# An S4 convolution and a GeGLU layer in one kernel: dt's broadcast, the order of exponentials, the table of a tanh, and a new order of steps

## The chip, the core and the metric

The kernel runs on one core of a Trainium2 chip. The core has a matrix engine (TensorE, PE in the profile, its weight loads as PEld), a vector engine (VectorE, DVE), an activation engine (ScalarE, ACT), GpSimd (POOL) and SyncE (SP), which here issues nearly all DMAs. Each engine works off its own instructions in order and waits on semaphores of the others. The metric is the device time of one execution in microseconds; times are medians of several runs. A time "at 165.68" is counted from the start of the profiled execution's span.

## The reference

Two branches are computed from the same input `x = u` (2048 positions, 640 channels) and mixed by a gate:

```python
g = sigmoid((x * gate_w).sum(-1, keepdims=True))
# branch a: a long convolution, one kernel of 2048 taps per channel
dt = exp(log_dt)[:, None]; A = A_re + 1j*A_im
P = exp((dt*A)[:, :, None] * l)                  # channel, state, tap
K = einsum("dn,dnl,dn->dl", C, P, dt*B).real
y = irfft(rfft(pad(u)) * rfft(pad(K)))[:L] + u * Dskip
# branch b: the feed-forward layer, 1728 hidden features
b = (gelu(x @ w_gate) * (x @ w_up)) @ w_down     # tanh form of gelu
out = g * y + (1 - g) * b
```

## The kernel before, in words

**Powers and taps.** The 2048 taps of the convolution kernel are products of a coarse and a fine factor, `eA` (21 exponents) and `eB` (32 exponents), for 128 states in partitions. Their sizes are exponentials of `a32[:, 0]` = dt times A's real part and of `a32[:, 1]`, which is twice that: `exps` (line 362) takes exponents in pairs (v, 2v) in one instruction where both are wanted, and alone where not. Their angles are phases made on DVE (`trig`, tile `ph`) and sines made on ACT (tile `T`). `ktable` multiplies size and angle on DVE; `contract` sums over the states on PE (tiles `cv`, evicted to `Kraw`), and `gather` turns the result round through memory (`Kd`) into `KTt`. The five parts of 128 channels are worked in groups of 2, 2 and 1.

**The start.** `scaled_a` (line 326) loads the exponential's table, spreads `log_dt` over 128 partitions by two matmuls with a row of ones, takes dt as the exponential of this, brings both halves of A into place by ten matmuls each with the identity, and multiplies. `turn_x` turns the first half of x on PE; the second half is brought by transposing loads that SP issues (`load_x`).

**Feed-forward.** `ffn_up` (line 619) makes a block of both projections, 10 matmuls of 512 columns, in one of two PSUM tiles `gu`; its copy to one of three tiles `GU` is done by ACT or DVE, and `send` stores it to `GUd` in memory. There are 54 such blocks, put between the steps of the tap tables. Later `glu_load`, `gelu`, `glu` (a multiply on DVE) and `down` (28 matmuls per block of 128 positions) take them up again. The down weights `Wd` are loaded in two halves; the first half lies where part 4's `Kraw` was.

**Convolution.** It goes through Fourier windows as matmuls: `u_forward` and `k_forward` (evicted by steps V and Q to `Uf` and `Kf`), `products` on DVE (`Ma`, `Mb`, `Tp`), `inverse` on PE, and `unfold`, which adds the skip term and branch b, scales by the gate and stores. All PSUM tiles `cv` are two buffers.

**The gate.** `gate` (line 649) makes 16 columns of logits, and takes the sigmoid as a tanh on ACT followed by a short chain on DVE, which gives `g32` and `rat`.

**What sets the order.** `ORDER` (line 36) is a list of 530 steps written out by hand: a letter for the kind, then part or row block, then index, and for evictions the engine (A for ACT, D for DVE, M for half each). `u` is the next up-projection, `p` its copy, `o` its store, `W` the next weight load, `e` exponentials, `t` phases and sines, `q` tap tables, `c` contraction, `C` its eviction, `w` the gather, `K`/`Q` and `U`/`V` the forward windows and their evictions, `P` products, `I`/`J` the inverse, `D`/`d` the down-projection and its eviction, `l`/`b` loads of the stored blocks, `G`/`g` gelu and multiply, `h` the gate, `L` a half of the down weights, `m` a Fourier matrix. The steps are issued in this order, and a scheduler then places each engine's instructions where it finds room, unless a dependency holds them. `table` chains all ACT instructions that need a table in the order of the list, `first` does the same for the first steps on DVE.

```python
b32 = pp.tile([N, D], FP32, name="b32")
def scaled_a():
    table(... InstLoadActFuncSet(..., act_func_set_id=6))
```

Of the kernel before, what the change touches and what calls it, by code (L numbers as in the profile page):

```python
# [9 lines left out]
ALU = mybir.AluOpType  # L10
# [23 lines left out]


ORDER = """
s a M W e04 i2 x01D e02 n M W e00 e03 i0 x00D x02D x10D e13 x12A u e01 pD u pA v o o x11A S0 S1 e05 u W r0 pD u pD u
e15 o pA o u pD u o e12 pA i1 r1 u u pD u m m o u t04 u o y3 u pD u o pD o o pD pD o o u r2 u pD W y2 pD o o k pD u o
e10 pA u W u e11 o e14 t05 y4 u !0 pA pA pA o o o t07 u pA q05 u u u pA pA W o pA o o t02 pA t06 q07 u t00 o q06 u y0
pA t01 t03 q01 pD q00 o y1 o o u pA q02 o W q04 q03 u pD t14 o u c02 t10 t16 u pA o c00 pD u pD c10 C00A c01 u !1 pA o  # L40
C02A c11 W o o q10 u C01D C10A m u C11D w0 u pA pA c12 C12A w1 o m u W pA m pA o o u u o t11 pA q11 o W u t17 t15 e24
u pA u o pD u o pD u pA W o o pD q17 u pD u e21 q15 u W o pA e22 u e25 q16 e23 o e20 pD o o pD o pA t13 o q14 t12 q12
m m u q13 c20 C20A u c22 pA c21 C21D t20 c30 m m c32 !2 C32A C22A pA C30A t21 u c31 m f0 m w2 C31A o q20 t22 F0P t23
U00 U03 U01 V01A u w3 o V03A V00A q22 q23 pD o U02 h K00 Q00D pA K02 q21 Q02D K03 u K01 V02A Q03A c40 C40A Q01D f1 pA
o !3 W b00 F1P c41 l00 G00 u L0 C41D pA c42 o l01 C42A l10 b01 w4 g00 b10 b11 P00 P01 U10 V10A u P02 U12 V12A f2 pA u
o o pA U13 K10 K12 Q12A Q10A V13A P03 u K11 G01 U11 pA L1 V11A F2A K13 Q13A Q11A K20 D00 g01 D01 Q20A P10 K22 K21 Q21A
U20 d01A U22 V20A Q22A P11 d00A l11 U23 V22A K23 D02 V23A f3 l20 Q23A d02D G10 g10 F3A I00 U21 U30 P12 V30A U33 o o
D03 G11 V21A U31 D10 I10 V33D d10A f4 D11 b20 d03A V31A U32 z00D g11 d11A D13 K30 d13A I01 z10A F4A Q30A K32 b21 V32A
K31 Q32A P20 P21 D12 l21 d12A G20 P22 Z00A P23 Q31A l30 Z01A g20 D20 U40 G21 z01A P13 d20D K40 I11 g21 V40A K42 z11A
Q40A K41 b30 G30 D21 I20 U42 D23 Q41A d23A K33 d21A K43 Q33M l31 Q43A D22 d22A P30 Z02A g30 U41 b31 Q42M G31 g31 D30  # L50
V41D I21 U43 V42A z20D V43D d30A P31 P32 D32 z21A d32A I30 P33 P40 z30A D31 J33 j33D d31A D33 J32 d33A Z03A P41 Z11A
P42 J41 j41A J40 P43 j40A j32A Z12A Z10A Z20D J43 J42 j43D Z21D j42A Z22M Z23D Z13D
"""


# [1 line left out]
def kernel(  # L57
# [18 lines left out]
    nc = tc.nc  # L76
# [12 lines left out]
    NM = 4  # L89
    DH = D // 2  # L90
    tt = nc.vector.tensor_tensor
# [55 lines left out]
    ident = cp.tile([128, 128], BF16, name="ident")  # L147
# [81 lines left out]
    ldt = pw.tile([1, D], BF16, name="ldt")  # L229
    ones = pw.tile([1, N], BF16, name="ones")  # L230
# [93 lines left out]
    b32 = pp.tile([N, D], FP32, name="b32")  # L324

    def scaled_a():
        table(nc.scalar.add_instruction(mybir.InstLoadActFuncSet(
            name=nc.get_next_instruction_name(), engine=mybir.EngineType.Activation, act_func_set_id=6)))
        pL = psC.tile([128, 2, 512], FP32, name="cv")
        pL = pL[:].rearrange("p e x -> p (e x)")[:, 0:D]  # L330
        for sl in (slice(0, 512), slice(512, D)):
            nc.tensor.matmul(pL[:, sl], lhsT=ones[:], rhs=ldt[:, sl], start=True, stop=True)
        table(nc.scalar.activation(out=dtb[:], in_=pL, func=ACT.Exp))
        pA = []
        for t in (Are_n, Aim_n):
            p = psF.tile([128, 2, 512], FP32, name="gu")
            pA.append(p[:].rearrange("p e x -> p (e x)")[:, 0:D])
            col = pA[-1].rearrange("n (p k) -> n k p", k=KT_)
            for k in range(KT_):
                n = (511 - k) // KT_ + 1  # L340
                for sl in (slice(0, n), slice(n, 128)):
                    nc.tensor.matmul(col[:, k, sl], lhsT=t[:, k], rhs=ident[:, sl], start=(k == 0), stop=True,
                                     skip_group_check=True)
        first(tt(out=a32[:, 0], in0=pA[0], in1=dtb[:], op=ALU.mult))
        first(nc.vector.tensor_scalar(out=a32[:, 1], in0=a32[:, 0], scalar1=2.0, scalar2=None, op0=ALU.mult))  # L345
        first(nc.vector.scalar_tensor_tensor(out=b32[:], in0=pA[1], scalar=TURN / (2.0 * math.pi), in1=dtb[:],
                                             op0=ALU.mult, op1=ALU.mult))
# [14 lines left out]
    def exps(p0, np_, y):  # L362

        dA, dB = tabs[p0 // 2]
        sl = slice(p0 * DP, (p0 + np_) * DP)
        if y == 0:
            nc.gpsimd.memset(dB[:, 0:np_, :, SLOT[0], :], 1.0)
        if y == 4:
            nc.gpsimd.memset(dA[:, 0:np_, 0, :], 1.0)
        jobs = jobs_b[6 * y:6 * y + 6] if y < 4 else jobs_a[7 * (y - 4):7 * (y - 3)]  # L370
        for xs, scale in jobs:
            n = len(xs)
            xsl = slice(xs[0], xs[-1] + 1, max(1, xs[-1] - xs[0]))
# [6 lines left out]
            table(nc.scalar.activation(out=dst, in_=src, func=ACT.Exp, scale=float(scale)))  # L380
# [174 lines left out]
    def dinv(m, r, e):  # L555
        return DFT[:, 2 + m // 2].rearrange("p r f -> p (r f)")[:, 512 * (m % 2) + 256 * r + 128 * e:][:, 0:128]
# [92 lines left out]
    def gate():  # L649
        pG = psC.tile([128, 2, 512], FP32, name="cv")  # L650
        for x in range(16):
            for kt in range(KT_):
                nc.tensor.matmul(pG[:, 0, x:x + 1], lhsT=xt_tile(kt, x // 4, x % 4), rhs=gwc[:, kt:kt + 1],
                                 start=(kt == 0), stop=(kt == KT_ - 1))
        glog = cp.tile([128, 16], BF16, name="glog")
        nc.scalar.copy(out=glog[:], in_=pG[:, 0, 0:16])
        gth = cp.tile([128, 16], FP32, name="gth")
        table(nc.scalar.activation(out=gth[:], in_=glog[:], func=ACT.Tanh, scale=0.5))
        g_bf = cp.tile([128, 16], BF16, name="g_bf")
        nc.vector.tensor_scalar(out=g_bf[:], in0=gth[:], scalar1=0.5, scalar2=0.5, op0=ALU.mult, op1=ALU.add)  # L660
# [133 lines left out]
    def products(part, j):  # L794
        mp = pools["mp"]
        if j == 0:
            pst[part] = (mp.tile([128, 2, 2, 2, 512], BF16, name="Ma"),
# [2 lines left out]
        Ma, Mb, T = pst[part]  # L800
# [10 lines left out]

        def join(M, c0, c1):
            tt(out=M[:, c0:c1, 0, 0], in0=M[:, c0:c1, 0, 0], in1=M[:, c0:c1, 1, 1], op=ALU.subtract)
            tt(out=M[:, c0:c1, 0, 1], in0=M[:, c0:c1, 0, 1], in1=M[:, c0:c1, 1, 0], op=ALU.add)

        last = part == NP - 1
        if j == 0:
# [18 lines left out]
    def inverse(part, c0, nc_):  # L836
# [12 lines left out]
        o = DP * (part - ZG[z][0])  # L849
        pY = psC.tile([128, 2, 512], FP32, name="cv")  # L850
        cs = slice(c0 % 2, c0 % 2 + nc_)
        for c in range(c0, c0 + nc_):
            for r in range(2):
                for e in range(2):
                    for m in range(NM):
                        nc.tensor.matmul(pY[:, c % 2, 256 * r + 128 * e:256 * r + 128 * (e + 1)], lhsT=dinv(m, r, e),  # L856
                                         rhs=pst[part][c // 2][:, c % 2, 0, r, 128 * m:128 * (m + 1)],
                                         start=(m == 0), stop=(m == NM - 1))
# [32 lines left out]
    pst = {}  # L891
# [44 lines left out]
    for step in ORDER.split():  # L936
# [3 lines left out]
        eng = step[-1]  # L940
# [101 lines left out]
        elif kind == "Q":  # L1042
            k_out(x, y, eng)
        elif kind == "P":
            products(x, y)
        elif kind == "l":
            glu_load(x, y)
        elif kind == "b":
# [47 lines left out]
```

## Time and profile before

| What | Value |
|---|---|
| Median of 3 runs | 319.92 us (319.89 to 319.99) |
| The profiled execution | 320.46 us |
| its span, first to last instruction | 318.5 us |
| PE busy | 292.6 us (92%) |
| DVE busy | 295.1 us (93%) |
| ACT busy | 249.1 us (78%) |
| DMA | 51.40 MB, 161 GB/s on the mean |
| table loads on ACT | 9, of 1.28 us each |

The profiled execution is one run with the hardware profiler; its 320.46 us hold the span and 1.96 us around it. The chain of waits goes back from the last instruction to what released each step; its shares are PE 38%, DVE 27%, ACT 18%, DMA 8%. A matmul's end is modelled, so that matmuls in a row overlap in the list: one row of 10 matmuls tells more by its length over all than by the time of one. In a timeline row stand the start, the length, the engine, the line, the operation, the tiles (written <- read), the shapes, the count, and in brackets how long the engine was idle before it and what ended that.

### The profile page before, as it was taken

The numbers are of one execution on the slowest core, as the hardware profiler recorded it, in microseconds if no ns is written. First come the engines' busy times: TensorE is split into PE (matmuls) and PEld (weight loads), VectorE is DVE, ScalarE is ACT, GpSimd is POOL, SyncE is SP. The second block draws the span as 40 slices with busy tenths as digits, with TensorE's granted clock in tenths as the row PEclk, the third lists the DMA queues.
The fourth block names the chain that finished last, engine by engine and source line by source line (L and its number), as shares of the span: only waits on it lengthen the run. The fifth ranks groups of instructions, "written<-read, shape, count | busy, mean of one in ns | idle before, by whom it ended". The sixth has DMA issues, their size and how long they took to land.

```text
span 318.5 us, 6270 instructions
## 1 busy us (share of the span) xinstructions
PE 292.6 (92%) x2432; PEld 182.0 (57%) x2463; DVE 295.1 (93%) x416; ACT 249.1 (78%) x351; POOL 14.4 (5%) x78
## 2 busy tenths in 40 slices
PE   4399999999999999999998889999989999999994
PEld 3243444444555444454475667676677877687773
DVE  3985999999998999999889999999989999999964
ACT  5989999999898899998999768926596738542750
POOL 7720000000000000000000000000000000000000
PEclk9999999999999999999999999999999999999999
DMA  7997456656627795454594699847826352900233
GB/s 220 167 245 220 155 182 209 214 161 215 182 71 164 205 278 182 154 111 127 104 283 137 117 321 232 233 115 182 228 63 172 87 147 70 263 2 0 56 97 82
DMA packets 102543, 51.40 MB, mean 161 GB/s; under 512 B 44081, under 2 KB 95730, under 8 KB 102514
## 3 DMA queue, kind: packets, MB, share of 16 engines
q1 hardware_dynamic: 102256, 50.48, 59.2%
q0 software_dynamic: 256, 0.53, 0.6%
q8 instruction: 19, 0.31, 0.4%
q14 instruction: 10, 0.08, 0.1%
q10 hardware_dynamic: 2, 0.00, 0.0%
HBM read 30.86 MB, written 18.16 MB: 154 GB/s over the span
## 4 chain that ended last, share of the span: by engine, by line
PE 38%; DVE 27%; ACT 18%; DMA 8%; issue 7%; SPq 1%; DVEq 0%; ACTq 0%
PE gu L788 17%; DVE ph L408 5%; PE cv L856 4%; PE gu L627 4%; DVE GU L127 3%; DVE ph L416 3%; PE cv L712 3%; PE cv L729 3%; ACT GU L123 3%; DVE sB L584 2%; DMA Wd<-in_B_w_down_dram 2%; DMA HT<-GUd 2%; ACT T L424 2%; PE cv L878 2%; DVE eB L585 2%
## 5 line engine op out<-in xcount | busy, mean ns | idle before, releaser
L627 PE MATMUL gu<-xT,W 128*128 128x512 bf16 x523 | 121.8, 382 | 4.0 <-ACT GU L123 1.4
L627 PEld LDWEIGHTS <-W 128*128 128x128 bf16 x540 | 52.2, 98 | 70.1 <-issue 12.5
L788 PE MATMUL gu<-Wd,HT 128*128 128x320 bf16 x448 | 64.4, 299 | 0.8 <-DMA Wd<-in_B_w_down_dram 0.8
L788 PEld LDWEIGHTS <-HT 128*128 128x128 bf16 x448 | 43.5, 98 | 18.6 <-issue 0.9
L424 ACT ACTIVATE T<-ph 128x1024 bf16<-128x1024 int16 (+3 forms) x40 | 46.4, 1196 | 2.6 <-DVE ph L408 1.5
L123 ACT CAST GU<-gu 128x1024 bf16<-128x1024 f32 (+1 forms) x33 | 32.3, 981 | 4.0 <-PE gu L627 3.8
L805 DVE TENSOR_TENSOR Tp<-Uf,Kf 128x6144 bf16<-128x6144 bf16 (+2 forms) x15 | 34.3, 2284 | 0.1
L772 ACT ACTIVATE HT<-HT 128x1792 bf16<-128x1792 bf16 x16 | 26.5, 1693 | 7.3 <-DMA HT<-GUd 7.3
L810 DVE TENSOR_TENSOR Mb<-Mb,Tp 128x4096 bf16<-128x4096 bf16 (+1 forms) x15 | 28.9, 1929 | 0.2
L127 DVE CAST GU<-gu 128x1024 bf16<-128x1024 f32 (+1 forms) x23 | 26.8, 1166 | 1.5 <-DMA GUd<-GU 1.0
L729 PE MATMUL cv<-KTt,DFT 128*128 128x128 bf16 x280 | 24.2, 219 | 1.9 <-ACT Kf L125 1.1
L125 ACT ACTIVATE ob<-gu,rat 128x640 bf16<-128x640 f32 x14 | 11.1, 792 | 18.5 <-PE gu L788 18.5
L380 ACT ACTIVATE eB<-a 128x256 bf16<-128x256 f32 (+2 forms) x63 | 23.3, 452 | 0.0
L729 PEld LDWEIGHTS <-DFT 128*128 128x128 bf16 x280 | 21.0, 98 | 2.0 <-issue 0.7
L123 ACT CAST Uf<-cv 128x1024 bf16<-128x1024 f32 x17 | 16.9, 1019 | 5.8 <-PE cv L712 3.7
L712 PE MATMUL cv<-pm,DFT 128*128 128x512 bf16 x72 | 19.5, 378 | 1.6 <-ACT Uf L123 0.8
L856 PEld LDWEIGHTS <-DFT 128*128 128x128 bf16 x320 | 18.8, 98 | 1.4 <-DVE HT L129 0.3
L408 DVE SCALAR_TENSOR_TENSOR ph<-b,phi 128x256 int32<-128x256 f32 (+1 forms) x63 | 19.4, 371 | 0.0
L125 ACT ACTIVATE Kf<-cv 128x512 bf16<-128x512 f32 x32 | 17.2, 597 | 2.8 <-PE cv L729 2.6
L729 PE MATMUL cv<-KTt,ME 128*128 128x128 bf16 x120 | 18.6, 219 | 0.0
L777 DVE TENSOR_TENSOR HT<-HT,Ut 128x1792 bf16<-128x1792 bf16 x16 | 17.0, 1083 | 1.2 <-ACT HT L772 0.9
L380 ACT ACTIVATE eA<-a 128x256 bf16<-128x256 f32 (+2 forms) x42 | 15.2, 444 | 1.9 <-DVE a L345 1.9
(184 smaller groups left out, 453.2 us busy)
## 6 DMA issues: line engine op xcount, KB each, us to landing
GUd<-GU SPq DMA_DIRECT2D x52, 256.0 KB, 2.7
HT<-GUd SPq DMA_DIRECT2D x16, 448.0 KB, 4.8
Ut<-GUd SPq DMA_DIRECT2D x16, 448.0 KB, 4.9
W<-in_B_w_gate_dram SPq DMA_DIRECT2D x12, 320.0 KB, 3.7
W<-in_B_w_up_dram SPq DMA_DIRECT2D x12, 320.0 KB, 4.3
fo<-in_A_u_dram SPq DMA_DIRECT2D x20, 128.0 KB, 3.1
out_dram<-GU SPq DMA_DIRECT2D x8, 256.0 KB, 2.4
T<-in_A_u_dram SPq DMA_DIRECT2D x2, 640.0 KB, 7.1
```

The costliest lines, as they stand in the source:

```text
L123: nc.scalar.copy(out=dst, in_=src)
L127: nc.vector.tensor_copy(out=dst, in_=src)
L380: table(nc.scalar.activation(out=dst, in_=src, func=ACT.Exp, scale=float(scale)))
L408: nc.vector.scalar_tensor_tensor(out=ph[:, x, :], in0=b32[:, dsl], scalar=float(A_OF[x0 + x] + MID), in1=phi[:, dsl], op0=ALU.mult, op1=AL ...
L424: table(nc.scalar.activation(out=dst, in_=phl, func=ACT.Sin, scale=-SIN_SCALE if r and x1 > NA else SIN_SCALE))
L627: nc.tensor.matmul(p[:, r], lhsT=W[:, kt, f0:f0 + 128], rhs=xT[:, kt, 512 * c:512 * (c + 1)], start=(kt == 0), stop=(kt == KT_ - 1))
L712: nc.tensor.matmul(pU[:, ri], lhsT=dmat(e, ri, m), rhs=pm[:, ri, e].rearrange("p c d -> p (c d)"), start=(e == 0), stop=(e == 1))
L729: nc.tensor.matmul(pW[:, ri, 128 * m:128 * (m + 1)], lhsT=lhs, rhs=rhs, start=(first and x == 0 and m == 0), stop=(x == len(seq) - 1), ski ...
L788: nc.tensor.matmul(pD[:, h, 0:DH], lhsT=HT[:, ft, 128 * e:128 * e + 128], rhs=Wd[ft // 7][:, ft % 7, DH * h:DH * (h + 1)], start=(ft == 0) ...
L805: tt(out=dst.rearrange("p c h r f -> p (c h) r f"), in0=U[:, c0:c1].rearrange("p c h f -> p (c h) f")[:, :, None, :].to_broadcast([128, n, ...
L810: tt(out=M, in0=M, in1=T[:, t0:t1], op=ALU.add)
L856: nc.tensor.matmul(pY[:, c % 2, 256 * r + 128 * e:256 * r + 128 * (e + 1)], lhsT=dinv(m, r, e), rhs=pst[part][c // 2][:, c % 2, 0, r, 128 ...
```

## The change

It does five things.

1. In `scaled_a`, every matmul that brings A into place gets a dependency on the last of dt's two matmuls, so that PE does these first. On PE, the ten matmuls of A's real part stood ahead of dt's in the old order, and stand behind them in the new one.
2. In `exps`, the jobs of a step are sorted by length: exponents that go alone are done ahead of the pairs.
3. In `gate`, table set 11 is loaded explicitly ahead of the tanh. The load that stood ahead of the first gelu is not there any more.
4. `products` gets the engine letter. With A the second half of a join is left out, and the inverse takes twice as many matmuls for that half in its place; the list has D with all 20 products, so that the joins and the matmuls are what they were.
5. `ORDER` is a new list of the same 530 steps. The evictions of two down-projection blocks, d23 and d30, go from ACT to DVE; of Q42, Q43 and Q33, one is split between the engines where two were. The contraction c11 stands behind two more up-projections on PE; part 4's third K window by index (K42) stands ahead of U's first transform (U40); stores, weight loads, gathers and copies stand a few places earlier or later.

```diff
+    def load_set(x):
+        table(nc.scalar.add_instruction(mybir.InstLoadActFuncSet(
+            name=nc.get_next_instruction_name(), engine=mybir.EngineType.Activation, act_func_set_id=x)))
...
     def scaled_a():
-        table(nc.scalar.add_instruction(mybir.InstLoadActFuncSet(
-            name=nc.get_next_instruction_name(), engine=mybir.EngineType.Activation, act_func_set_id=6)))
+        load_set(6)
...
-            nc.tensor.matmul(pL[:, sl], lhsT=ones[:], rhs=ldt[:, sl], start=True, stop=True)
+            spread = nc.tensor.matmul(pL[:, sl], lhsT=ones[:], rhs=ldt[:, sl], start=True, stop=True)
...
-                    nc.tensor.matmul(col[:, k, sl], lhsT=t[:, k], rhs=ident[:, sl], start=(k == 0), stop=True,
-                                     skip_group_check=True)
+                    inst = nc.tensor.matmul(col[:, k, sl], lhsT=t[:, k], rhs=ident[:, sl], start=(k == 0), stop=True,
+                                            skip_group_check=True)
+                    tc.add_manual_dep(inst.ins, spread.ins.name, mybir.DependencyInfo(
+                        mybir.DependencyClass.NoSync, mybir.DependencyReason.DATA), reason="dt goes first")
...
-        for xs, scale in jobs:
+        for xs, scale in sorted(jobs, key=lambda job: len(job[0])):
...
         gth = cp.tile([128, 16], FP32, name="gth")
+        load_set(11)
         table(nc.scalar.activation(out=gth[:], in_=glog[:], func=ACT.Tanh, scale=0.5))
...
-            tt(out=M[:, c0:c1, 0, 1], in0=M[:, c0:c1, 0, 1], in1=M[:, c0:c1, 1, 0], op=ALU.add)
+            if eng != "A":
+                tt(out=M[:, c0:c1, 0, 1], in0=M[:, c0:c1, 0, 1], in1=M[:, c0:c1, 1, 0], op=ALU.add)
```

Of the list, the places that the prediction speaks of (old, then new):

```diff
-C02A c11 W o o q10 u C01D C10A m u C11D w0 u pA pA c12 C12A w1
+o o q10 u C01D C02A C10A m u c11 C11D w0 u o pA pA c12 m o u C12A W w1
...
-P13 d20D K40 I11 g21 V40A K42 z11A Q40A K41 b30
+K42 U40 G21 z01A K40 P13D d20D I11 g21 V40A z11A Q40A K41 b30
...
-Q41A d23A K33 d21A K43 Q33M l31 Q43A D22 d22A P30 Z02A g30 U41 b31 Q42M G31 g31 D30
+Q41A K33 d23D K43 d21A Q33A l31 Q43M P30D D22 d22A Z02A Q42A g30 U41 P31D b31 D30
...
-V41D I21 U43 V42A z20D V43D d30A P31 P32 D32
+V41D I21 G31 V42A U43 z20D V43D d30D g31 z21A P40D D32
```

More of the change, by code (lines that the diff above doesn't have):

```diff
@@ L36 @@
 ORDER = """
[L37 to L51, printed above, removed]
@@ L792, in down, with products @@
                                            rat[:, 4 * c + k:4 * c + k + 1])
-    def products(part, j):
+    joined = {}
+    def products(part, j, eng):
         mp = pools["mp"]
@@ L813, in join @@
             tt(out=M[:, c0:c1, 0, 0], in0=M[:, c0:c1, 0, 0], in1=M[:, c0:c1, 1, 1], op=ALU.subtract)
-            tt(out=M[:, c0:c1, 0, 1], in0=M[:, c0:c1, 0, 1], in1=M[:, c0:c1, 1, 0], op=ALU.add)
+            if eng != "A":
+                tt(out=M[:, c0:c1, 0, 1], in0=M[:, c0:c1, 0, 1], in1=M[:, c0:c1, 1, 0], op=ALU.add)
+            for c in range(c0, c1):
+                joined[part, c + (2 if M is Mb else 0)] = eng != "A"
         last = part == NP - 1
@@ L853, in inverse @@
             for r in range(2):
+                halves_of = ((0, r),) if r == 0 or joined[part, c] else ((0, 1), (1, 0))
                 for e in range(2):
                     for m in range(NM):
-                        nc.tensor.matmul(pY[:, c % 2, 256 * r + 128 * e:256 * r + 128 * (e + 1)], lhsT=dinv(m, r, e),
-                                         rhs=pst[part][c // 2][:, c % 2, 0, r, 128 * m:128 * (m + 1)],
-                                         start=(m == 0), stop=(m == NM - 1))
+                        for h in halves_of:
+                            nc.tensor.matmul(pY[:, c % 2, 256 * r + 128 * e:256 * r + 128 * (e + 1)],
+                                             lhsT=dinv(m, r, e),
+                                             rhs=pst[part][c // 2][:, c % 2, h[0], h[1], 128 * m:128 * (m + 1)],
+                                             start=(m == 0 and h[0] == 0),
+                                             stop=(m == NM - 1 and h == halves_of[-1]))
         pend["j" if nc_ == 1 else "z", part, c0 if nc_ == 1 else c0 // 2] = lambda eng: copy(
@@ L1044 @@
         elif kind == "P":
-            products(x, y)
+            products(x, y, eng)
         elif kind == "l":
```

17 lines of the change are left out of this document (16 added, 1 removed).

## The prediction

> **What bounds the kernel now.** I read the page first, then stages, then the chain of waits, then each place where the diff moves something.
>
> ```profile
> span 318.5 us, 6270 instructions
> PE 292.6 (92%) x2432; PEld 182.0 (57%) x2463; DVE 295.1 (93%) x416; ACT 249.1 (78%) x351; POOL 14.4 (5%) x78
> ...
> 102.00:144.00 42.00, 40.44 (x249) 19.28 (x251) 41.76 (x74) 39.23 (x65) 0.36 (x2) 1.00 0.67 185
> 144.00:164.00 20.00, 19.61 (x194) 10.20 (x195) 18.43 (x40) 19.54 (x22) 0.00 (x0) 1.00 0.62 148
> ...
> 171.00:191.00 20.00, 16.85 (x217) 12.60 (x221) 19.91 (x13) 14.59 (x21) 0.00 (x0) 1.00 0.75 193
> ...
> 236.00:300.00 64.00, 63.38 (x632) 48.60 (x638) 63.79 (x50) 37.07 (x53) 0.00 (x0) 1.00 0.37 100
> ```
>
> The stage rows give length, then busy time of PE, weight loads, DVE, ACT, POOL, then PE's granted clock (1.00 throughout). No single engine bounds: three are nearly full from 102 on, and which is fullest changes: DVE from 102 to 144, ACT from 144 to 164, DVE in 171 to 191 (PE idles 3.15 there), PE and DVE together from 236 on. A gain passes to the end only if the engine that is full behind it moves too.
>
> **The change, part by part.** Against the old program, the new one has the same PE, POOL and SP instructions; ACT has one table load fewer; DVE has two more evictions of the down-projection and one less of K. What changes is order. Although all products now carry a "D", each joins as before: that edit costs nothing, being decided while the program is built.
>
> *dt ahead of A.*
>
> ```profile
> 3.20 1.25 PE L342 MATMUL gu<-ident,Are_n 128*128 128x103 bf16 x10 [3.20 <-DMA Are_n<-in_A_A_re_dram]
> 3.21 1.28 ACT L327 ACT_TABLE_LOAD   x1
> 4.38 0.71 PE L332 MATMUL cv<-ldt,ones 1*128 1x512 bf16 x2
> 5.13 0.70 ACT L333 ACTIVATE dtb<-cv 128x640 bf16<-128x640 f32 x1 [0.64 <-PE cv L332]
> 5.87 0.82 DVE L344 TENSOR_TENSOR a<-gu,dtb 128x640 f32<-128x640 f32 x1 [3.45 <-ACT dtb L333]
> 7.76 3.11 ACT L380 ACTIVATE eA<-a 128x512 bf16<-128x512 f32 x7 [1.93 <-DVE a L345]
> ```
>
> dt's exponential waited 0.64 for PE, after the table load ended at 4.49. With dt's two matmuls first (3.20 to 3.91) and A's ten behind (to 5.16), the exponential runs 4.49 to 5.19 and `a` starts at 5.23 instead of 5.87: 0.64 earlier. ldt's landing has no row. It had landed by 4.38 (no DMA wait there); then A's matmuls would end at 6.34 and `a` start near 6.36, 0.5 later. Its issue begins with that of Are_n and it is far smaller, so I take 0.64 early; ends: 0.64 early, 0.5 late. By the arbitration that the Trainium skill gives (DMA: Bandwidth & Descriptors, section Queues, rings and completion order), each DMA engine takes turns between queues packet by packet, so a load on ACT's own queue need not stand behind SP's bulk loads; no row here shows it.
>
> Single exponentials first: they need only the first half of `a`, so ACT starts at about 6.1, not 7.76, another 1.0 on ACT alone. It buys nothing at the next meeting point, where ACT already waits for PE:
>
> ```profile
> 13.87 10.39 SPq L208 DMA_TRANSPOSE xT<-in_A_u_dram  x5
> 22.93 1.01 ACT L123 CAST GU<-gu 128x1024 bf16<-128x1024 f32 x1 [0.92 <-PE gu L627]
> 24.37 4.08 SPq L638 DMA_DIRECT2D GUd<-GU  x3
> 29.67 1.22 DVE L127 CAST GU<-gu 128x1024 bf16<-128x1024 f32 x1 [1.03 <-DMA GUd<-GU]
> 30.95 2.32 PE L627 MATMUL gu<-xT,W 128*128 128x512 bf16 x10 [0.27 <-DVE GU L127]
> 33.59 6.63 PE L627 MATMUL gu<-xT,W 128*128 128x512 bf16 x29
> 35.94 1.01 ACT L123 CAST GU<-gu 128x1024 bf16<-128x1024 f32 x1
> ```
>
> PE and DVE carry 0.64 as far as the fourth up-projection's copy. That copy needs the first of three GU buffers back, and the first store cannot be issued before SP has worked off five transposing loads, at 24.37, which depend on nothing that moves. So 29.67 stays, the sixth up-projection stays at 30.95, and the seventh at 33.59 behind it. ACT, up to 0.64 early, meets that one at 35.94 and waits. What the start gains becomes longer waits at 29.67 and 30.95. Later covers: ACT keeps perhaps 0.05. I count 0.05; ends 0.5 lost, 0.64 gained.
>
> *Contraction c11 behind two more up-projections.*
>
> ```profile
> 94.00 0.20 PE L601 MATMUL cv<-eA,eB 128*128 128x84 bf16 x1 [0.38 <-DVE Kraw L129]
> ...
> 101.23 0.20 PE L601 MATMUL cv<-eA,eB 128*128 128x84 bf16 x1
> ...
> 100.19 1.11 ACT L125 ACTIVATE Kraw<-cv,ksign 128x1008 bf16<-128x1008 f32 x1
> ...
> 102.19 0.96 DVE L578 TENSOR_TENSOR Q<-T,eA 128x1536 bf16<-128x1536 bf16 x1 [1.15 <-PE cv L603]
> ```
>
> PE waited 0.38 before c11 for an eviction to free its buffer; with up-projections first it works on, and c12 (the block at 101.23), with the same work ahead of it, comes up to 0.38 earlier. c12 also needs c10's eviction (100.19 to 101.30), ahead of which ACT now moves one up-projection copy. DVE waited 1.15 for c12, so it moves as c12 does. I take 0.3; ends 0 and 0.38. It passes on: DVE is full to 144, ACT (behind DVE) to 164. The other reorderings up to there (two sine tables in a row, an eviction ahead of a copy near 136, gathers not split by a store) swap neighbours of about 1.0 each (the copies above) that run anyway; I count 0 and allow 0.3 either way, the size of the c11 term.
>
> *One table for tanh and gelu.*
>
> ```profile
> 159.47 1.17 SPq L758 DMA_DIRECT2D HT<-GUd  x2
> ...
> 165.45 0.21 ACT L658 ACTIVATE gth<-glog 128x16 f32<-128x16 bf16 x1
> 165.68 1.28 ACT L772 ACT_TABLE_LOAD   x1
> 166.97 3.29 ACT L772 ACTIVATE HT<-HT 128x1792 bf16<-128x1792 bf16 x2
> ...
> 172.68 0.38 PE L684 MATMUL cv<-fo,flip 128*128 128x512 bf16 x1 [0.55 <-ACT Kf L125]
> ...
> 165.69 0.17 DVE L660 TENSOR_SCALAR g_bf<-gth 128x16 bf16<-128x16 f32 x1 [0.36 <-ACT gth L658]
> ...
> 176.75 0.96 ACT L125 ACTIVATE Kraw<-cv,ksign 128x840 bf16<-128x840 f32 x1 [1.00 <-PE cv L603]
> ...
> 182.99 0.38 SPq L929 DMA_DIRECT2D Wd<-in_B_w_down_dram  x1
> ...
> PE gu L788 <- DMA Wd<-in_B_w_down_dram: 0.8, 1, 0.8
> ```
>
> The gelu moves from 166.97 to 165.68: 1.29 on ACT. PE takes at most the 0.55 that it waited for ACT at 172.68; the fold's copies and the last eviction of Kraw (176.75), each behind PE, then come about 0.5 earlier. On that eviction hang SP's gathers of part 4, behind them the first half of the down weights (their memory is Kraw's), and for these PE waited 0.8 at the first down-projection. So 0.5 of 1.29 reaches 190. DVE saves 0.36: the gate's first step now stands behind an eviction and a product. Ends: 0 (DVE, full in 171 to 191, is not ahead, or the gelu's loads land late) and 1.29.
>
> The Trainium skill (ScalarE: Activation LUTs, section What ACT_TABLE_LOAD costs) adds a drain of 1.38 us to each load. Here the gelu starts 0.01 after the load's end; by the page ACT would gain 2.66 and, PE's wait being 0.55, the sum would keep its 0.5 while its upper end would rise to 2.66.
>
> *Two evictions of the down-projection from ACT to DVE.*
>
> ```profile
> L129 DVE TENSOR_SCALAR ob<-gu,rat 128x640 bf16<-128x640 f32 x2 | 1.8, 876 | 0.0
> L129 DVE TENSOR_SCALAR Kf<-cv 128x512 bf16<-128x512 f32 x8 | 5.2, 673 | 0.0
> ...
> 279.48 1.08 DVE L777 TENSOR_TENSOR HT<-HT,Ut 128x1792 bf16<-128x1792 bf16 x1
> ...
> 281.27 3.97 PE L788 MATMUL gu<-Wd,HT 128*128 128x320 bf16 x28
> ...
> 304.93 0.42 DVE L814 TENSOR_TENSOR Mb<-Mb 128x512 bf16<-128x512 bf16 x1
> ...
> 308.59 1.07 PE L856 MATMUL cv<-Mb,DFT 128*128 128x128 bf16 x16
> ```
>
> DVE gains 2 x 0.88 - 0.67 = 1.09 of work late, where it is full. The first multiply of the last GLU comes 0.88 - 0.67 = 0.21 later against the rest and is needed by PE at 281.27, 0.71 after its end at 280.56. The very last products end at 305.35, 3.2 ahead of their matmuls. So it is hidden behind PE's down-projections: 0; uncovered, 1.09. ACT, with room there, gains nothing that counts.
>
> **The sum.** 0.05 + 0.30 + 0.50 = 0.85. The profiled execution took 320.46, 1.96 more than its span of 318.5; it becomes 319.6. The median of the three runs, 319.92, lies 0.54 below the profiled one; the same 0.85 off gives 319.1.
>
> **The rivals.**
>
> *The start comes through.* If SP's first store lands earlier, or ACT's lead is worth more than the copy's delay, 0.64 in place of 0.05: 319.1 - 0.6 = 318.5. For it: the chain of waits begins in just this exponential. Against it: the 1.03 at 29.67, a DMA's.
>
> *The gate's 0.5 is absorbed.* DVE, full from 171 to 191, evicts the last-but-one Kraw block before PE can go on; if only it counts, or the gelu's loads (issued from 159.47) land after 165.7, the 0.5 shrinks to 0.1 or less. With c11's gain also eaten: 319.92 - 0.3 = 319.6. The Trainium skill's page ScalarE: Activation LUTs (section Table sets: the hidden batching unit) lists tanh beside exp and sigmoid and not beside the gelu in use here; by it the load would have to stay, and the gate would give nothing. The rows before the change show two loads and so cannot tell.
>
> *dt ahead of A does not do what it says.* If ldt lands last, `a` is 0.5 late, ACT's full stretch passes it on, and 0.35 of the sum is left: 319.92 - 0.35 = 319.6.
>
> *Slower: K's third window ahead of U's first transform.*
>
> ```profile
> 248.38 1.70 ACT L772 ACTIVATE HT<-HT 128x1792 bf16<-128x1792 bf16 x1
> ...
> 249.81 1.03 PE L712 MATMUL cv<-pm,DFT 128*128 128x512 bf16 x3
> ```
>
> In part 4 the K window now takes one of the two evicting buffers ahead of U at 249.81, and the next window waits until ACT has copied it out, behind the gelu half of 248.38. Today that half ends at 250.08. The window, 16 matmuls of 128 columns, should take U's 1.03 (4 of 512, the same columns), so it ends near 250.8; its two evictions, at most 0.67 each by the DVE row, end near 252.1; and PE, with U and two of the 28 down-projection matmuls (0.28) in between, needs the buffer at 252.1. It decides from a gelu half that ends more than about 0.7 later against PE; then PE waits for what is over, at most a whole half, 1.70. The price is 1.70 on the spot: 319.1 + 1.7 = 320.8. For it: ACT's gelu halves hang on HT loads, PE's order does not. Against it: ACT is little used there (37.07 of 64).
>
> **How the numbers follow.** My forecast, start absorbed and the rest as summed, gets 0.45 and 319.1, with its own range 318.8 to 319.4. The start coming through, 0.17 (318.5). The gate absorbed, 0.20 (319.6), in which the page's rule has 0.02. ldt late, 0.06 (319.6). Slower by K's window, 0.12 (320.8). A difference under 0.2%, 0.64 us, is about what a measurement of this kernel cannot tell from none: faster is under 319.28, slower over 320.56. Faster: 0.17 and 0.40 of the forecast's 0.45, together 0.57. The same: 0.05, 0.20, 0.06, together 0.31. Slower: 0.12. The range of 8 in 10 takes in the start coming through, with a little more for the reorderings' 0.3 (318.2), and the absorbed cases with the same 0.3 and part of the slower one (320.3).
>
> **What would show it.** Right: dt's exponential at 4.5 with no wait for PE and `a` at 5.2; the fourth copy still near 29.7, its wait for the store grown to about 1.6; no wait ahead of c11, DVE's wait for c12 about 0.8; one table load ahead of the gate, the gelu 1.3 earlier against it; the wait at 172.68 gone; the first down-projection about 0.85 earlier; PE not waiting for the multiplies of the last GLU. Wrong: a fourth copy that comes 0.6 earlier (the start came through); a new wait of PE for DVE in 171 to 191; PE waiting for a gelu half near 250; or a DVE from 236 on that holds PE up by about 1.

## The result, and the profile after

| | before | changed |
|---|---|---|
| median of 16 runs each | 319.69 us (318.44 to 320.27) | 318.16 us (317.05 to 319.43) |
| ratio, 95% interval | | 0.996, 0.9946 to 0.9973 |
| profiled execution, its span | 320.46, 318.5 | 319.25, 317.1 |

The changed kernel is faster by 0.4%: 319.69 x 0.004 = 1.28 us, by the interval 0.86 to 1.73; the medians differ by 1.53. The prediction was 319.1, 0.85 lower, with a range from 318.2 to 320.3; the ratio, on the 319.92 that it counted from, gives 318.64. The spans differ by 1.4, but the runs of one kernel spread over some 2 us, so two single traces are a weak ground. Their sections, read along the span, come first.

The timeline of the changed kernel at the start (start, length, engine, line; in brackets the idle time before, and what ended it):

```profile
2.47 0.71 PE L335 MATMUL cv<-ldt,ones 1*128 1x512 bf16 x2 [2.47 <-DVE ones L235]
4.50 0.70 ACT L336 ACTIVATE dtb<-cv 128x640 bf16<-128x640 f32 x1
5.23 0.83 DVE L349 TENSOR_TENSOR a<-gu,dtb 128x640 f32<-128x640 f32 x1 [2.82 <-ACT dtb L336]
...
20.49 1.23 DVE L131 CAST GU<-gu 128x1024 bf16<-128x1024 f32 x1 [0.51 <-PE gu L632]
22.65 1.01 ACT L127 CAST GU<-gu 128x1024 bf16<-128x1024 f32 x1 [1.92 <-PE gu L632]
23.82 4.36 SPq L643 DMA_DIRECT2D GUd<-GU  x3
28.28 1.22 DVE L131 CAST GU<-gu 128x1024 bf16<-128x1024 f32 x1
...
33.31 7.07 PE L632 MATMUL gu<-xT,W 128*128 128x512 bf16 x32 [0.38 <-ACT GU L127]
35.67 1.01 ACT L127 CAST GU<-gu 128x1024 bf16<-128x1024 f32 x1
```

dt's exponential waits for nobody and `a` comes at 5.23, as predicted. But the fourth copy comes at 28.28, not at 29.67, and does not wait for the store, which SP issued 0.55 earlier. ACT's copy at 35.94 moved to 35.67: 0.27 came through.

The same view around c11, the gate and the first down-projection:

```profile
100.42 0.20 PE L606 MATMUL cv<-eA,eB 128*128 128x84 bf16 x1
101.37 0.96 DVE L583 TENSOR_TENSOR Q<-T,eA 128x1536 bf16<-128x1536 bf16 x1 [0.91 <-PE cv L608]
...
163.54 1.28 ACT L108 ACT_TABLE_LOAD   x1
164.84 0.21 ACT L664 ACTIVATE gth<-glog 128x16 f32<-128x16 bf16 x1
164.96 3.27 ACT L778 ACTIVATE HT<-HT 128x1792 bf16<-128x1792 bf16 x2
...
175.62 0.97 ACT L129 ACTIVATE Kraw<-cv,ksign 128x840 bf16<-128x840 f32 x1 [1.00 <-PE cv L608]
176.15 1.89 PE L718 MATMUL cv<-pm,DFT 128*128 128x512 bf16 x8 [0.57 <-DVE Kraw L133]
...
182.10 0.38 SPq L944 DMA_DIRECT2D Wd<-in_B_w_down_dram  x1
...
190.34 1.93 PE L794 MATMUL gu<-Wd,HT 128*128 128x320 bf16 x13 [1.15 <-DMA Wd<-in_B_w_down_dram]
```

c12 (100.42) and DVE's Q behind it are now 0.82 early; there is no wait ahead of c11. One table load serves tanh and gelu, and the gelu runs at 164.96. Kraw's last eviction is 1.13 early, PE's next transform, now 0.57 behind DVE's eviction of Kraw, only 0.78, and the first down-projection, 1.15 behind the down weights, 0.40. In the kernel before, the up-projection ahead of c11 (ten matmuls, of which nine have a record) and that transform were:

```profile
91.31 2.32 PE L627 MATMUL gu<-xT,W 128*128 128x512 bf16 x9
...
176.93 1.67 PE L712 MATMUL cv<-pm,DFT 128*128 128x512 bf16 x7 [0.22 <-DVE Kraw L129]
```

Then this, in the kernel before and in the changed one:

```profile
231.07 3.29 ACT L772 ACTIVATE HT<-HT 128x1792 bf16<-128x1792 bf16 x2 [1.31 <-DMA HT<-GUd]
```

```profile
229.29 3.28 ACT L778 ACTIVATE HT<-HT 128x1792 bf16<-128x1792 bf16 x2
```

The kernel before waited 1.31 for an HT load here, the changed one not at all. Behind this place the changed trace is 1.36 ahead, ahead of it 0.39: 0.97 of the 1.40 at the end arose at one transfer that no edit touches. The experiments had to show whether that is the change or the execution.

### The profile page after: what moved, and what is told of

It is laid out like the page before. It is cut to its first block, busy times and chain, and to the rows that moved or that the text cites. A ratio compares the mean times of both kernels' runs of the same rounds, so it can differ in the third digit from the quotient of the medians.

```text
span 317.1 us, 6300 instructions
## 1 busy us (share of the span) xinstructions
PE 294.0 (93%) x2463; PEld 182.0 (57%) x2463; DVE 296.2 (93%) x417; ACT 246.9 (78%) x349; POOL 14.2 (4%) x78
## 4 chain that ended last, share of the span: by engine, by line
PE 47%; DVE 22%; ACT 14%; DMA 8%; issue 5%; SPq 2%; DVEq 0%; ACTq 0%
PE gu L794 15%; PE gu L632 8%; PE cv L869 6%; DVE ph L413 5%; PE cv L735 4%; PE cv L718 4%; DMA Wd<-in_B_w_down_dram 3%; ACT eA L385 2%; ACT eB L385 2%; PE cv L893 2%; DMA T<-in_A_u_dram 2%; DMA Kd<-Kraw 2%; DVE ph L421 2%; DVE eB L590 1%; DVE sB L589 1%
## 5 line engine op out<-in xcount | busy, mean ns | idle before, releaser
L632 PE MATMUL gu<-xT,W 128*128 128x512 bf16 x540 | 123.7, 383 | 2.8 <-ACT GU L127 1.7
L129 ACT ACTIVATE ob<-gu,rat 128x640 bf16<-128x640 f32 x12 | 9.5, 795 | 18.3 <-PE gu L794 18.3
```

Source lines behind the costliest of these rows:

```text
L129: nc.scalar.activation(out=dst, in_=src, func=ACT.Copy, scale=scale)
L632: nc.tensor.matmul(p[:, r], lhsT=W[:, kt, f0:f0 + 128], rhs=xT[:, kt, 512 * c:512 * (c + 1)], start=(kt == 0), stop=(kt == KT_ - 1))
```

## The experiments

Each was timed in five rounds beside the kernel before. Left, per run, the time; right, what its profile shows: the start of ACT's copy near 80 us, the distance from there to DVE's Q behind c12, the distance from DVE's Fourier step (153.58 before) to Kraw's last eviction, PE's wait for Wd, ACT's wait for HT near 231, the span.

| kernel | median | ratio, 95% interval | copy | to Q | to Kraw | Wd | HT | span |
|---|---|---|---|---|---|---|---|---|
| before | | | 80.14 | 22.05 | 23.17 | 0.76 | 1.31 | 318.5 |
| before again | 319.59 | 1.0008, 0.9987 to 1.0029 | 80.01 | 22.04 | 23.17 | 0.60 | 0.57 | 317.7 |
| gate only | 318.49 | 0.9984, 0.9961 to 1.0008 | 79.45 | 22.04 | 22.65 | 1.12 | 0 | 317.0 |
| list only | 319.02 | 0.9998, 0.9974 to 1.0022 | 80.31 | 21.51 | 23.17 | 1.42 | 0.26 | 317.8 |
| start only | 319.20 | 0.999, 0.9973 to 1.0006 | 79.22 | 22.06 | 23.17 | 0.66 | 0.35 | 317.4 |
| dt only | 318.99 | 0.9988, 0.997 to 1.0005 | 79.58 | 22.04 | 23.17 | 0.52 | 1.09 | 317.6 |
| code only | 318.60 | 0.9978, 0.9958 to 0.9999 | 79.09 | 22.05 | 22.65 | 0 | 0.21 | 315.5 |
| no gate | 318.35 | 0.9958, 0.9941 to 0.9975 | 80.06 | 21.51 | 23.17 | 1.31 | 0 | 317.7 |
| changed | 318.16 | 0.996, 0.9946 to 0.9973 | 79.86 | 21.51 | 22.65 | 1.15 | 0 | 317.1 |
| changed again | 318.11 | 0.9954, 0.9937 to 0.9971 | 79.05 | 21.51 | 22.65 | 0.55 | 0.13 | 315.7 |
| warm | 317.55 | 0.9945, 0.9918 to 0.9971 | 78.02 | 21.51 | 23.37 | 0.28 | 0.73 | 316.7 |
| warm again | 318.14 | 0.9959, 0.9939 to 0.9978 | 78.83 | 21.50 | 22.86 | 0.88 | 0 | 316.5 |
| later | 318.41 | 0.9962, 0.9943 to 0.9982 | 78.83 | 21.52 | 22.65 | 0.31 | 0.60 | 315.5 |
| warm and later | 317.43 | 0.994, 0.9918 to 0.9962 | 77.48 | 21.52 | 22.88 | 0.21 | 0 | 315.6 |

Two columns hardly scatter and follow the edits: the distance to Q is 21.50 to 21.52 wherever the new list is and 22.04 to 22.06 elsewhere; the distance to Kraw is 23.17 without the gate's edit, and 22.65 with it, but for the three kernels with added matmuls. The copy near 80, Wd and HT scatter by about a microsecond under one and the same code.

**The kernel before, unchanged.**

> The kernel before, unchanged, as a measure of what one execution differs from the next. In the two traces at hand the change is 0.39 us ahead at the down-projections of 200 to 225, and 1.33 ahead after 232: there the kernel before waited 1.31 on ACT (at 231.07) for an HT load issued at 223.87, and the changed one did not wait. Theory L (that wait is one execution's luck): a second profile of the kernel before shows under 0.5 of it, and its span is about 318.5 - 0.9 = 317.6. Theory S (the wait belongs to the old order): it is there again, 1.0 to 1.5, and the span is 318.5 within 0.3. By both the ratio to the kernel before is 1.000 within 0.0015.

```profile
23.50 4.82 SPq L638 DMA_DIRECT2D GUd<-GU  x3
28.43 1.22 DVE L127 CAST GU<-gu 128x1024 bf16<-128x1024 f32 x1
35.81 1.01 ACT L123 CAST GU<-gu 128x1024 bf16<-128x1024 f32 x1
...
230.26 3.28 ACT L772 ACTIVATE HT<-HT 128x1792 bf16<-128x1792 bf16 x2 [0.57 <-DMA HT<-GUd]
```

The HT wait is 0.57, 0.74 of those 0.97 are gone, and the span is 317.7: between the two theories, nearer to luck. Over all fourteen profiles this wait is 1.31 and 1.09 in two, 0.73 at most in the rest, and 0 in five. So most of what separates the two traces at 231 belongs to one execution. In the mean it is 0.60 without the gate's edit (six profiles) and 0.21 with it (eight); whether the edit has a part in that stays open. The fourth copy is at 28.43 with no wait: the first store went out at 23.50, though nothing ahead of it differs.

**The gate's table alone.** One edit:

```diff
         gth = cp.tile([128, 16], FP32, name="gth")
+        table(nc.scalar.add_instruction(mybir.InstLoadActFuncSet(
+            name=nc.get_next_instruction_name(), engine=mybir.EngineType.Activation, act_func_set_id=11)))
         table(nc.scalar.activation(out=gth[:], in_=glog[:], func=ACT.Tanh, scale=0.5))
```

> The kernel before with one edit: the gelu's table is loaded ahead of the gate's tanh, so that one table load (1.28 us) goes. The prediction: the gelu is 1.3 earlier, the wait of 0.55 at 172.68 goes, the first down-projection (190.74) comes 0.5 earlier and the time is 0.5 lower (ratio 0.9984). Rival (the down weights take it back): the gelu is 1.3 earlier, Kraw's last eviction and the issue of Wd 0.3 to 0.5 earlier, but PE then waits that much longer than 0.76 for Wd at the first down-projection, which stays at 190.7 within 0.2; ratio 1.000 within 0.001. Rival (tanh is not to be had from that table): the program loads tanh's table besides, two loads, nothing earlier.

```profile
175.55 0.97 ACT L125 ACTIVATE Kraw<-cv,ksign 128x840 bf16<-128x840 f32 x1 [1.00 <-PE cv L603]
181.43 0.38 SPq L931 DMA_DIRECT2D Wd<-in_B_w_down_dram  x1
...
190.24 1.93 PE L790 MATMUL gu<-Wd,HT 128*128 128x320 bf16 x13 [1.12 <-DMA Wd<-in_B_w_down_dram]
```

Kraw comes 0.52 earlier against the Fourier step (22.65 for 23.17). Wd is issued 1.56 earlier than before (181.43 for 182.99), of which 0.69 is the start of this execution, yet it takes 8.8 us to land, not 7.7; PE waits 1.12 and starts 0.50 early. That is the 0.5 expected, but less than the 0.69 that this execution was ahead from its start: measured from there, the rival holds in this profile, and the weights take it back. What else moves at that time shows in the stages of the kernel before and of the changed one (length; busy PE, weight loads, DVE, ACT, POOL; clock, DMA share, GB/s):

```profile
184.00:188.00 4.00, 3.41 (x40) 2.38 (x39) 4.00 (x5) 3.62 (x7) 0.00 (x0) 1.00 1.07 321
188.00:192.00 4.00, 3.25 (x46) 2.78 (x44) 4.00 (x5) 0.40 (x1) 0.00 (x0) 1.00 1.18 315
```

```profile
184.00:188.00 4.00, 3.47 (x50) 2.78 (x49) 4.00 (x4) 3.39 (x5) 0.00 (x0) 1.00 1.05 320
188.00:192.00 4.00, 2.85 (x35) 2.27 (x33) 4.00 (x4) 0.11 (x1) 0.00 (x0) 1.00 1.19 303
```

The DMA engines count as busy throughout from 184 to 192 (share 1.05 to 1.19) at 300 to 320 GB/s, with Wd, HT and Ut loads under way together. That these crowd each other is a likely reason why an earlier issue need not land as much earlier; no run tests it, and in code only, below, a Wd issued 2.09 earlier than before took 7.5 to land. In the time, gate only is 0.9984 with an interval that reaches past 1: not settled by it.

**The list alone.** The kernel before with the new `ORDER`.

> The kernel before with the new list alone: c11 behind two more up-projections, the K window ahead of U40, d23 and d30 on DVE; dt, the exponentials and the gate as before. The prediction: no wait ahead of c11 (0.38 today), DVE's Q behind c12 0.3 earlier, first down-projection 0.3 earlier, time 0.3 lower (ratio 0.999). Rival (c11 is worth more): Q 0.5 earlier, as the changed kernel's trace has it (0.28 ahead before c11, 0.82 behind), and 0.5 of it in the time (0.9984). Rival (the list pays later than 190): first down-projection within 0.2 of 190.74, but past 232 the trace is ahead by 0.8 or more and the ratio is 0.997. Slower by K's window: PE waits near 250 for an eviction behind a gelu half, ratio over 1.002.

```profile
100.87 0.20 PE L601 MATMUL cv<-eA,eB 128*128 128x84 bf16 x1
101.82 0.96 DVE L578 TENSOR_TENSOR Q<-T,eA 128x1536 bf16<-128x1536 bf16 x1 [0.90 <-PE cv L603]
```

From the copy at 80 to Q it is 0.54 shorter (21.51 for 22.05): the rival, c11 is worth more than 0.3, and more than the 0.38 given as its upper end. The last-but-one stage adds 0.04 (ahead by 0.66 at the down-projection's eviction of 242.50, by 0.70 at the end), and no wait of PE near 250 appears. The first down-projection came 0.31 late, behind a Wd wait of 1.42, so that no gain reached it in this profile, and the time is 0.9998 with an interval that holds the 0.54 (0.9983) as well as nothing.

**All code edits with the old list** (the changed kernel with the old `ORDER`).

> The changed kernel with the old list: dt ahead of A, singles first, one table for tanh and gelu; every place in the list as before. The prediction: 0.05 from the start and 0.5 from the gate, 0.55 lower (ratio 0.9983); the fourth up-projection's copy stays near 29.7 with its wait for the first store at about 1.6. Rival (the start comes through in part): the fourth copy comes at about 28.3 as in the changed kernel's trace, the ACT copy at 35.94 moves to 35.67, 0.28 stays to the end, and the time is 0.8 lower (0.9975). Rival (the down weights take both back): first down-projection at 190.74 less 0 to 0.3, ratio 0.999 to 1.000.

The fourth copy came at 28.09 after a wait of 0.49 for the store, ACT's copy at 34.90, 1.04 early; the first down-projection found its weights there and was 2.14 early. The ratio, 0.9978, lies between the prediction's and the rival's.

**The start, in three steps.** dt ahead of A with singles first, dt ahead of A alone, and the changed kernel without the gate's edit:

> The kernel before with dt ahead of A and singles first, nothing else. The four profiles with the old start show ACT's copy at 80.14 at 80.14, 80.01, 79.45 and 80.31 (mean 79.98, a spread of 0.9 with nothing changed there), and the first store issued anywhere from 22.61 to 24.37; the two with the new start 79.86 and 79.09 (mean 79.48). The prediction (the start is absorbed at the fourth copy by the first store's landing): `a` 0.64 earlier, the fourth copy waits for the store, the copy at 80.14 no earlier than the old mean, 80.0 within 0.3; ratio 0.9998. Rival (the first store was late in one execution only; what is left of `a` passes): no wait for the store or a short one, the copy at 79.5 within 0.4, ratio 0.9985. By the clock (PE's first up-projections run at 0.427 us a matmul and later at 0.216; the change between the two comes at 18.4 to 20.4 and does not follow the kernel): half of `a`'s 0.64 passes, 79.7.

> The kernel before with dt ahead of A alone; the exponentials in pairs first as before. The prediction said that singles first buy nothing: then ACT's wait ahead of its first copy is about 0.9 to 1.0 shorter than in start_only and the changed kernel (1.20 to 1.92 there), the copy is set by PE all the same, and the start's worth is that of start_only: the copy at 80 us at 79.5 within 0.4, ratio 0.9985 to 0.999. Rival (singles first carry part of it): ACT becomes the bound ahead of its first copy (no wait there), and the copy at 80 us is at 80.0.

> The changed kernel with the gate's two table loads back (tanh loads its own table, the gelu its own): start and list new, gate old. Prediction: the changed kernel less the gate's 0.5: 0.35 below the kernel before (0.9989). Rival (the gate's gain is taken back at the down weights): no different from the changed kernel, 0.996 within the interval; the gelu comes 1.3 later against the gate's product, the wait of 0.55 ahead of the fold is back, Kraw's last eviction is 0.5 later against DVE's ME step, and PE's wait for Wd at the first down-projection is shorter by as much.

Start only, then dt only:

```profile
21.54 1.01 ACT L123 CAST GU<-gu 128x1024 bf16<-128x1024 f32 x1 [1.20 <-PE gu L629]
28.76 1.23 DVE L127 CAST GU<-gu 128x1024 bf16<-128x1024 f32 x1 [1.51 <-DMA GUd<-GU]
35.03 1.01 ACT L123 CAST GU<-gu 128x1024 bf16<-128x1024 f32 x1 [0.42 <-PE gu L629]
```

```profile
21.91 1.01 ACT L123 CAST GU<-gu 128x1024 bf16<-128x1024 f32 x1 [1.02 <-PE gu L629]
```

In start only the fourth copy does wait for the store, 1.51, and ACT's copy behind it then waits 0.42 for PE: what the prediction described, but worth 0.42 there and not the whole. In both profiles the copy near 80 (79.22 and 79.58) is where the rival "what is left of `a` passes" puts it; both time intervals (0.999 and 0.9988) hold the prediction's 0.9998 as well as the rival's 0.9985. Two spacings hold in every one of the fourteen profiles, to 0.02: ACT's copy near 36 comes 13.02 behind its first copy, or 6.27 behind the fourth copy, whichever is later (22.65 to 35.67; 28.76 to 35.03). In the profile before, both gave 35.94 (22.93 + 13.01; 29.67 + 6.27): the store was exactly on the edge. Without singles first ACT still waited 1.02 ahead of its first copy, so they buy nothing at this point; the wait was expected to shrink by 0.9 to 1.0, and against start only it shrank by 0.18. No gate has the changed kernel's time (0.9958 beside 0.996), which speaks for the rival, that the gate's gain is taken back; but its wait for Wd is 1.31, not shorter than the changed kernel's 1.15, so that the way in which the rival saw this happen is not shown.

**The changed kernel again.**

> The changed kernel again: a second profile, and the ratio again. If the profiles of one kernel differ by when transfers land and not by their engines' work, then from ACT's copy at 80 us to DVE's Q behind c12 this profile has the same distance as the first changed one (101.37 - 79.86 = 21.51, against 22.05 of the kernel before), and from the gate on the same distance to Kraw's eviction, while the first down-projection's wait for Wd is anywhere between 0 and 1.4 and the HT load near 231 is waited for by 0 to 1.3. Ratio 0.996 within 0.0015.

The distances are the same to 0.01, the waits are not, and the span is 315.7, 1.4 below the first profile.

**PE kept at work ahead of the first up-projections.** Nine matmuls that nobody reads, behind the first block's last transposes:

```diff
+        if (q, i) == (0, 2):
+            warm = psF.tile([128, 2, 512], FP32, name="gu")
+            for y in range(9):
+                inst = nc.tensor.matmul(warm[:, y % 2], lhsT=ident[:], rhs=xn[0][:, y % 4, 0:512], ...)
...
```

> The changed kernel with nine more matmuls of 128x512 on PE, whose result nobody reads, between the transposes of the first and of the second block of x, where PE waits 4.7 us for DVE. Theory C (what the start gains is set by PE's half rate: the first up-projections take 0.427 us a matmul because PE stood idle before them): the up-projections run at 0.216 from the first, the first copy comes 1.5 to 2 earlier than 20.49, the copy at 79.86 by 0.5 to 1.5 earlier (then the first store's landing holds the fourth copy), time 0.5 to 1.5 lower than the changed kernel (0.992 to 0.995). Rival (the rate does not depend on what PE did before, or DVE's copies of x set the first up-projections): nothing moves, 0.996. Rival (the store takes it back): first copies earlier, the fourth copy waits 1 or more for the first store, the copy at 79.86 within 0.3.

> The changed kernel with the nine unread matmuls, again. Theory C (PE's half rate sets the first copies): first copy near 18.2, ACT's copy behind it and the copy at 80 us follow as far as the first store lets them: 13.02 behind ACT's first copy, or 6.27 behind the fourth copy, whichever is later (both spacings held in all profiles so far: 22.65 to 35.67, 21.88 to 34.90; and 28.76 to 35.03, 27.55 to 33.83). Time 0.5 below the changed kernel's 0.9957, so 0.994 within 0.002. Rival (what the start gains is eaten later): the time as the changed kernel's.

Timeline of the first up-projections in the changed kernel (with one stage), in warm, and in warm again (with two stages):

```profile
16.29 6.33 PE L632 MATMUL gu<-xT,W 128*128 128x512 bf16 x20
...
17.00:19.00 2.00, 2.00 (x6) 0.76 (x5) 1.97 (x3) 2.00 (x7) 0.96 (x8) 1.00 1.23 198
```

```profile
15.27 4.48 PE L638 MATMUL gu<-xT,W 128*128 128x512 bf16 x20
...
27.55 1.23 DVE L131 CAST GU<-gu 128x1024 bf16<-128x1024 f32 x1 [1.61 <-DMA GUd<-GU]
33.83 1.01 ACT L127 CAST GU<-gu 128x1024 bf16<-128x1024 f32 x1 [0.50 <-PE gu L638]
```

```profile
9.74 3.01 PE L259 MATMUL gu<-T,ident 128*128 128x512 bf16 x9
14.76 1.28 PE L255 MATMUL cv<-ident,T 128*128 128x128 bf16 x12 [2.02 <-DVE xT L266]
15.84 5.74 PE L638 MATMUL gu<-xT,W 128*128 128x512 bf16 x20
```

```profile
13.00:15.00 2.00, 0.24 (x5) 0.24 (x5) 2.00 (x7) 2.00 (x5) 2.00 (x4) 0.99 0.81 181
15.00:17.00 2.00, 2.00 (x14) 1.28 (x12) 1.39 (x4) 2.00 (x6) 2.00 (x5) 0.50 1.14 239
```

In warm, 20 matmuls take 4.48 (0.216 from start to start) where the changed kernel took 6.33; the copy near 80 is 1.84 earlier, though the fourth copy waits 1.61 for the store. So the half rate was what held the first copies, and it depends on what PE did before. Of the 1.84, 0.72 is gone again at Kraw's last eviction (23.37 for 22.65), where DVE waits 1.5 for ACT's sines and not 0.7; the times, 0.9945 and 0.9959, do not tell either run from the changed kernel. In warm again the nine matmuls were through at 12.75, PE then stood for 2.02, and the granted clock was 0.50 from 15 on: 5.74 for the 20. The idle time alone does not decide it: in warm and later, the last run below, PE stood for 2.58 and the 20 took 4.48. The Trainium skill (TensorE: Matmul & The Clock Gate, section Part 1: The HAM clock gate) says that the full rate is granted after a busy window of about 3.4 us that runs free of the kernel; the two runs agree, with a half clock in warm again that lasted 3.41 (14.97 to 18.38), and so does the place of the change of rate, which in the profiles without added matmuls lies anywhere between 18.1 and 20.9.

**Two transposing loads behind the first stores.** On SP, the fourth and fifth get a dependency on the third and fifth store; in the changed kernel, and in warm:

```diff
+        if len(loads) > 3:
+            tc.add_manual_dep(inst.ins, stores[(2, 4)[len(loads) - 4]].ins.name, ...)
```

> The changed kernel with only that move of two transposing loads. The first store goes out at about 20.5 to 21.5 and no longer at 22 to 24. If the prediction's premise holds (the first store's landing sets the start), the fourth copy comes without a wait, ACT's copy at 36 is 13.02 behind its first copy in this profile, and the time is 0 to 0.4 below the changed kernel's (0.9945 to 0.9957). Rival: nothing, since three of five profiles with the new start had no such wait that counts.

> As the one before, and on SP the fourth and fifth transposing load of x (for the second half of the rows) are issued behind the third and the fifth store, not ahead of the first. If the first store's landing holds the start, the fourth copy no longer waits (1.61 in the first profile with the nine matmuls), the copy at 33.83 comes 0.5 earlier, at 13.02 behind ACT's first copy, and the time is 0.993. Rival (ACT alone sets it): no difference to the run without this move. Slower: the transposing loads, some 2 us of SP each, now stand ahead of later stores, and a copy between 25 and 45 us waits for a store by over 1.

```profile
20.72 2.28 SPq L649 DMA_DIRECT2D GUd<-GU  x2
27.25 1.22 DVE L131 CAST GU<-gu 128x1024 bf16<-128x1024 f32 x1
34.64 1.01 ACT L127 CAST GU<-gu 128x1024 bf16<-128x1024 f32 x1
```

```profile
9.63 2.72 PE L265 MATMUL gu<-T,ident 128*128 128x512 bf16 x9
14.93 0.83 PE L261 MATMUL cv<-ident,T 128*128 128x128 bf16 x12 [2.58 <-DVE xT L272]
15.59 4.48 PE L644 MATMUL gu<-xT,W 128*128 128x512 bf16 x20
...
25.89 1.22 DVE L131 CAST GU<-gu 128x1024 bf16<-128x1024 f32 x1
33.29 1.01 ACT L127 CAST GU<-gu 128x1024 bf16<-128x1024 f32 x1
```

The fourth copy does not wait in either, and ACT's copy is at 13.02 behind its first (20.27 to 33.29): the 0.5 that the store took in warm is back. The move alone (later) has the changed kernel's time, 0.9962, as its rival had it. Warm and later has the lowest median, 317.43, and the best ratio, 0.994; its interval still overlaps the changed kernel's, so that it beats that one is likely and not shown.

## Why the prediction was right and wrong

**dt ahead of A: the step failed.** `a` 0.64 earlier was right, and that singles first buy nothing. Wrong was "So 29.67 stays": the five transposing loads depend on nothing that moves, but the first store behind them went out anywhere from 22.61 to 24.45 in the ten profiles without added matmuls or moved loads (the profile before had 24.37, nearly the latest). Where it was early, ACT's first copy set the start, and that one moved (22.77 in the mean of the four profiles with the old start, 22.11 in the six with the new one). Over the four profiles with the old start ACT's copy near 80 stands at 79.98 in the mean, over the six with the new one (moved loads and added matmuls left out) at 79.48: 0.5, with a scatter of 0.4 in each group, in place of 0.05. With so few profiles the 0.5 is uncertain by about 0.26, so it is likely and not certain. The times point the same way: from list only to no gate, which differ by the start's edits alone, the ratio goes from 0.9998 to 0.9958, and the two intervals hardly meet. It is the rival named "the start comes through". The sign given for it, an earlier fourth copy, was there (28.28), but by luck: the kernel before, unchanged, had 28.43 in its second profile.

**c11: the mechanism right, the size wrong.** 0.54 in place of 0.30, the same within 0.01 in all eight profiles with the new list. The bracket of 0.38 counts from the modelled end of the last matmul; ten matmuls from 91.31 at 0.216 would have let c11 start at 93.47, and it started at 94.00. A wait of PE read from its bracket is short by the overlap of the pipeline, 0.16 here. Some of it is given back: with both the new list and the new start, DVE waits 0.46 at 150.46 and loses 0.2. What that wait is for stays open; list only does not have it.

**One table: right up to Kraw, then two covers.** 0.52 at Kraw's eviction, in place of the 0.5 of the sum, in all five profiles that have the edit and no added matmuls. The rule that tanh would need another table, which the prediction took from the Trainium skill (ScalarE: Activation LUTs, section Table sets: the hidden batching unit), fell: one load served both. The drain that the Trainium skill gives (the same page, section What ACT_TABLE_LOAD costs) was not seen: tanh began 0.02 after the load's end. Then the step "So 0.5 of 1.29 reaches 190" failed twice. DVE's eviction of the other Kraw block held PE 0.57 instead of 0.22, a wait that the prediction had named as a sign against itself, and 0.35 of the 0.52 went there: this is its rival "the gate's 0.5 is absorbed", with 0.17 left where the rival had 0.1 or less. And the first down-projection starts when Wd lands, 7.5 to 8.8 behind its issue in the fourteen profiles. Against the Fourier step, it came 0.25 early in the mean of eight profiles with the edit and 0.13 late in six without: some 0.4, with a scatter of 0.4, of which 0.17 is what PE's transform kept. In the time none of it is seen (no gate, 0.9958, beside the changed kernel's 0.996).

**Evictions on DVE, and the K window: right.** From 242 to the end 0.04 is gained. In the changed profile the list of PE's waits from 236 on is empty, so the slower rival (1.70 at the gelu half) did not come.

**The sum.** 0.5 + 0.54 - 0.2 + 0.4 + 0.04 = 1.28 against 1.28 by the ratio and 0.85 predicted. That the terms fit so well is partly chance: two of them carry a scatter of 0.4, and with intervals of about 0.002 to either side the times show the change as a whole to be faster, not what each term brings. The median of 318.16 lies 0.9 below the 319.1: 0.43 of this is the sum, 0.23 is the base (the kernel before had a median of 319.92 in the three runs shown and 319.69 in sixteen), and most of the rest, 0.25, is that the medians differ by 1.53 where the ratio gives 1.28.

## What to carry to other kernels

A wait for a transfer that is read from one profile is one draw: before calling a landing fixed, ask what happens if it comes a microsecond earlier, and which engine would set the pace then. Compare two kernels by distances between steps of the same engines, of which the one around c11 repeats here to 0.02 us, and keep start, loads and weights apart from them. And take what an idle PE loses from the starts of its matmuls, not from the bracket.

## What was not expected of the hardware

The stage from 17 to 19 of the changed kernel shows a granted clock of 1.00 although its matmuls there stood 0.427 apart. In that trace the records of the clock begin only at 20.02, about where the spacing goes over to 0.216, and a stretch without a record counts as 1.00 in the view. In two of fourteen profiles, gate only and warm again, the first up-projections show the 0.50, and there records of the clock stand ahead of them. So the spacing of the matmuls tells the rate; a 1.00 at the start of a trace can also mean that nothing was recorded. The same load of Wd took 7.5 to 8.8 us to land in the fourteen profiles, and in gate only the issue that was 1.56 earlier landed 0.5 earlier.
